# Front of a linear-attention and routed-MoE kernel: results in a ring of two double banks, denominators as a 65th column, v cast by its load

## The chip, the cores and the metric

One NeuronCore of a Trainium2 chip runs the whole program. The metric is device time in microseconds, the median of three runs. Beside it stands one execution taken with the hardware profiler; all durations, waits and orders below are from that one. Engines are named as in the profile: PE is TensorE's matmul side and PEld its weight load, DVE is VectorE, ACT ScalarE, POOL GpSimd, SP the engine that only issues transfers.

## What is computed

Inputs q, k, v are (8, 8, 576, 64) fp32: 8 batches, 8 heads, 576 positions, 64 wide. The output of the attention, with the heads side by side, is 4608 tokens of 512, and goes through 8 experts whose weights per token come from eight rounds of row and column normalisation.

```python
def phi(x):
    return np.where(x > 0, x, np.exp(x) - 1.0) + 1.0
q_p, k_p = (phi(q), phi(k))
kv = np.einsum('bhsd,bhse->bhde', k_p, v)
z = np.sum(k_p, axis=2)
num = np.einsum('bhsd,bhde->bhse', q_p, kv)
den = np.einsum('bhsd,bhd->bhs', q_p, z)[..., None] + 1e-06
...
x = transposed(num / den)                  # (4608, 512)
P = np.exp(x @ w_gate - max)
for _ in range(8):
    P /= P.sum(1, keepdims=True) + 1e-09
    P /= P.sum(0, keepdims=True) + 1e-09
    P *= N / E
for e in range(E):
    out += P[:, e:e + 1] * (np.maximum(x @ w1[e], 0.0) @ w2[e])
```

## The kernel before

The program has two parts that overlap. The *front* computes the attention; the *experts* are the two matmul layers of the eight experts.

**Front.** The function `att(b, g)` (from L268) handles one *half batch*: four heads of one batch, numbered n = 2b + g from 0 to 15. Its steps, with the names of the profile:

- three loads into `kqin` (k and q) and `vin`, 576 KB each, two buffers deep (L283 to L298). Half batches 2 to 5 load through POOL's queue, the others through SP's.
- phi of k and q: exp on ACT into `e`, then on DVE max(x + 1, 1) into `t` and the minimum with `e` (L307, L320, L323).
- v is cast to fp16 into `vv`, whose 65th column is one, by ACT or DVE (L337). So the product k'v carries the sum of k' with it.
- `kv`: 18 matmuls into a double PSUM bank (L352); ACT or DVE evict it to `kvz`, masked to its diagonal blocks (L363, L365).
- `qt`: nine transposes of q' in two pieces of five and four (L380), copied out to `qpT` (L251 or L253).
- `den`: ten matmuls of two columns (L395); DVE adds epsilon and takes the reciprocal into `rden` (L401, L403).
- `num`: ten matmuls of 128 columns in three pieces (L419), each scaled by DVE with `rden` into `xn` (L424).
- `xt`: ten transposes of `xn` in two pieces (L435), copied out to `xT`, the tokens in the layout in which the experts read them (L439).

After each pair of batches 36 small matmuls make the gate's logits (`logits`, L447) and ACT their exp. When all are there, `sinkhorn` (L464) does the eight rounds on DVE, with one small matmul each (L493).

**PSUM.** The pools at L174 to L176 and L203 hold two single banks for layer 2 (`ye0`, `ye1`), two for layer 1 (`hq`), two that all of the front's results but `kv` share (`att`), and one double bank for `kv`. The first half batch borrows the `ye` banks for numerators. When the front is over, `f_close` (L563) frees its pools, and two fixed banks (`Zt`) take the place of the double bank.

**Experts.** Expert 0 runs alongside the front: tokens in nine groups of 512, layer 1 as plain matmuls for the first five groups (`layer1`, L608), ReLU on ACT, layer 2 in `unit_plain` (L877). The other groups, and all of experts 1 to 7, use a seven-product scheme with sums of blocks (`block7`, L755 and L760; `unit`, L1015). The blocks of x for it are formed on DVE (`x_blocks`), written to DRAM (`xd`) and read back per expert (`xs`). Weights are loaded and cast to fp16 through POOL's queue (`load_w`, L236), two buffers each for w1 and w2.

**Order.** Nothing is left to a scheduler at run time. Every step is registered with `add` or `fadd` and gets a number; at the end a list gives, engine by engine, the numbers in the order in which they are issued (L1116 to L1177). Each engine works its list in order, waiting at each step for its data and its buffer, so a step that waits holds up all that follow it on its engine. TensorE's list starts with dummy matmuls on a zeroed tile (`warm`, L527), which fill the time until inputs arrive. Costs beside `add` are for the planner that made the list and do nothing on the chip; so do dependencies that carry no data.

Of the kernel before, what the change touches and what calls it, by code (L numbers as in the profile page):

```python
# [10 lines left out]
FP32 = mybir.dt.float32  # L11
FP16 = mybir.dt.float16
# [127 lines left out]
def kernel(  # L140
# [10 lines left out]
    nc = tc.nc  # L151
# [24 lines left out]
    aps = ctx.enter_context(tc.tile_pool(name="aps", bufs=2, space=PSUM))  # L176
# [9 lines left out]
    NX = 5  # L186
    MG = 99
# [14 lines left out]
    vv_t = [fp.tile([P, 2, NJ, D + 1], FP16, tag=f"vv{i}", name=f"vv{i}", bufs=1) for i in range(2)]  # L202
    kvps = front.enter_context(tc.tile_pool(name="kvps", bufs=1, space=PSUM))  # L203
    diag = fp.tile([P, 2, D + 1], FP16, tag="diag", name="diag", bufs=1)
    half_ = fp.tile([P, 2], FP32, tag="half", name="half", bufs=1)
    p_kv = S_.pool(1)
# [3 lines left out]
    p_vv, p_kvz, p_qpT, p_xn, p_rden = (S_.pool(2) for _ in range(5))  # L210
# [50 lines left out]
    v_land, kv_id = [], []  # L261
# [6 lines left out]
    def att(b, g):  # L268
# [3 lines left out]
        def ps_home(i):  # L272
            if n < 1 and i < 2:
                return p_ye[i], yps, f"ye{i}"
            return p_att, aps, "att"

# [3 lines left out]
        for nm, ten in (("k", k), ("q", q), ("v", v)):  # L280
            gr = gin[nm] = S_.grp(p_in[nm]) if nm == "v" else gkq

            def fn(_, gr=gr, nm=nm, ten=ten):  # L283
                if nm == "v":
                    gr["tile"] = fp.tile([P, 2, NJ, D], FP32, tag="vin", name="vin", bufs=2)
                    dst = gr["tile"]
                else:
                    if nm == "k":
                        gr["tile"] = fp.tile([P, 2, 2, NJ, D], FP32, tag="kqin", name="kqin", bufs=2)
                    dst = gr["tile"][:, "kq".index(nm)]  # L290
                (nc.gpsimd if 2 <= n <= 5 else nc.sync).dma_start(
                    out=dst.rearrange("p r j d -> p r (j d)"),
                    in_=AP(tensor=ten.tensor, offset=(b * H + 4 * g) * S * D, ap=src))
            ti = fadd(("pool", 1.0) if 2 <= n <= 5 else ("sp", 0.45), fn, acq=[] if nm == "q" else [gr],
# [43 lines left out]
        tvv.append(fadd({"act": 1.15, "dve": 0.76}, f_v, deps=[ta, tin["v"]],  # L338
# [8 lines left out]
        def f_kv(_):  # L347
            gkv["tile"] = kvps.tile([P, 2, 512], FP32, tag="kv", name="kv_ps")
            for j in range(NJ):
                for hh in range(2):  # L350
# [3 lines left out]
                                     rhs=gvv["tile"][s, :, j, :], start=(j == 0), stop=(j == NJ - 1))  # L354
        kv_id.append(len(S_.t))
        tkv = fadd(("pe", 0.54), f_kv, deps=[tph["k"]] + tvv, acq=[gkv], use=[gvv, gt["k"]], prio=pr)
# [17 lines left out]
        for j0, j1 in ((0, 5), (5, NJ)):  # L374
            gp = S_.grp(p_att)

            def f_qt(_, j0=j0, j1=j1, gp=gp):
                gp["tile"] = aps.tile([P, 5, 2, PW], FP16, tag="att", name="qt_ps")
                for j in range(j0, j1):
                    nc.tensor.transpose(gp["tile"][:, j - j0, :, :].rearrange("p h w -> p (h w)"),  # L380
                                        gt["q"]["tile"][:, j, 2:4, :].rearrange("p r d -> p (r d)"), ident)

            def f_qc(e, j0=j0, j1=j1, gp=gp):
                copy(e, gq["tile"][:, :, j0:j1, :].rearrange("p h j w -> p j h w"), gp["tile"][:, 0:j1 - j0])
            t1 = fadd(("pe", 0.06 * (j1 - j0)), f_qt, deps=[tph["q"], tqa, t_init], acq=[gp], use=[gt["q"]], prio=pr)
# [3 lines left out]
        gden, grd, gxn = S_.grp(p_att), S_.grp(p_rden), S_.grp(p_xn)  # L389

        def f_den(_):
            gden["tile"] = aps.tile([P, 5, 2, 2], FP32, tag="att", name="den_ps")
            for i, j in enumerate(js):
                for hh in range(2):
                    nc.tensor.matmul(gden["tile"][:, i, :, hh],  # L395
                                     lhsT=gq["tile"][:, hh, j:j + 2, :].rearrange("p j w -> p (j w)"),
                                     rhs=gz["tile"][:, hh, :, D], start=True, stop=True)

        def f_rd(_):
            grd["tile"] = fp.tile([P, 5, 4], FP32, tag="rden", name="rden")  # L400
            nc.vector.tensor_scalar(out=grd["tile"], in0=gden["tile"].rearrange("p i r h -> p i (r h)"),  # L401
                                    scalar1=1e-6, scalar2=None, op0=ALU.add)
            nc.vector.reciprocal(grd["tile"], grd["tile"])  # L403
        tden = fadd(("pe", 0.26), f_den, deps=tq + tz, acq=[gden], use=[gq, gz], prio=pr)
        trd = fadd(("dve", 0.5), f_rd, deps=[tden], acq=[grd], use=[gden], prio=pr)

        def f_xa(_):
            gxn["tile"] = fp.tile([P, 5, 4, D], FP16, tag="xn", name="xn")
        txa = fadd(("none", 0.0), f_xa, deps=[tden], acq=[gxn], prio=pr)
        txn = []  # L410
        for i0, i1 in ((0, 2), (2, 4), (4, 5)):
            hn = ps_home(i0 // 2)
            gn = S_.grp(hn[0])

            def f_num(_, i0=i0, i1=i1, gn=gn, hn=hn):
                gn["tile"] = hn[1].tile([P, 2, 2, 2, D], FP32, tag=hn[2], name="num_ps")
                for i in range(i0, i1):
                    for hh in range(2):
                        nc.tensor.matmul(gn["tile"][:, i - i0, :, hh, :],  # L419
                                         lhsT=gq["tile"][:, hh, js[i]:js[i] + 2, :].rearrange("p j w -> p (j w)"),  # L420
                                         rhs=gz["tile"][:, hh, :, 0:D], start=True, stop=True)

            def f_xn(_, i0=i0, i1=i1, gn=gn):
                nc.vector.tensor_tensor(  # L424
                    out=gxn["tile"][:, i0:i1], in0=gn["tile"][:, 0:i1 - i0].rearrange("p i r h e -> p i (r h) e"),
                    in1=grd["tile"][:, i0:i1, :, None].broadcast_to([P, i1 - i0, 4, D]), op=ALU.mult)
# [783 lines left out]
```

## Time and profile before

| | us |
|---|---|
| three runs | 959.27, 959.45, 959.61 |
| median | 959.45 |
| profiled execution, whole | 958.96 |
| its span, first to last instruction | 957.0 |
| last matmul issued at | 952.6 |
| logits of the last batches | 129 |
| first matmul of expert 0 | 20.0 |

The page lists each engine's busy time, a chain of waits followed back from the last instruction, and groups of equal instructions. A group's row reads: line, engine, operation, output and input tiles with shapes, count, then total busy time and mean ns of one, then the engine's idle time just before and what ended it. A row in the order of time has start and length in us, then the same names, and in brackets the idle time before it. Matmuls are pipelined, so a row of several is longer than the distance to the next row; the distance between two starts is what the engine was held for.

### The profile page before, as it was taken

What the parts mean: (1) busy time and instruction counts of PE and PEld (TensorE: products, weight loads), DVE (VectorE), ACT (ScalarE), POOL (GpSimd) and SP (SyncE); (2) the same over time, 40 slices, a digit from 0 to 9 for tenths busy, and PEclk for the clock granted to TensorE, in tenths of its full rate; (3) what the DMA queues carried; (4) which work ended last, traced back from release to release, by engine and by line L of the source; (5) the groups of instructions that cost most, each with busy time, mean ns of one, the idle gap of its engine ahead of it and who ended that gap; (6) DMA issues with size and microseconds to landing.
All of it is one profiled execution on the core that took longest, in us unless ns stands there. A gap on an engine that the chain in (4) does not pass through costs nothing.

```text
span 957.0 us, 18776 instructions
## 1 busy us (share of the span) xinstructions
PE 950.7 (99%) x7265; PEld 649.8 (68%) x7265; DVE 768.8 (80%) x1526; ACT 571.7 (60%) x1035; POOL 152.5 (16%) x199
## 2 busy tenths in 40 slices
PE   9999999999999999999999999999999999999998
PEld 4566676566676667766676666766677666766676
DVE  6898888788887787888877788877878788877776
ACT  6798854667555555555555555555555555555552
POOL 3100000012112211221112211221112211111111
PEclk9999999999999999999999999999999999999999
DMA  9987855533345421544135431644225431425545
GB/s 315 310 313 257 217 155 169 133 88 89 89 140 118 108 71 52 121 111 100 56 99 110 110 88 47 149 103 108 61 61 112 111 99 57 138 78 155 154 105 133
DMA packets 109946, 121.83 MB, mean 127 GB/s; under 512 B 7840, under 2 KB 92960, under 8 KB 109856
## 3 DMA queue, kind: packets, MB, share of 16 engines
q1 hardware_dynamic: 84320, 96.23, 32.6%
q0 software_dynamic: 25136, 23.87, 14.5%
q8 instruction: 57, 0.93, 0.4%
q10 hardware_dynamic: 400, 0.52, 0.2%
q14 instruction: 33, 0.27, 0.1%
HBM read 119.69 MB, written 17.69 MB: 144 GB/s over the span
## 4 chain that ended last, share of the span: by engine, by line
PE 97%; DMA 1%; DVE 1%; ACT 1%; issue 0%; SPq 0%; DVEq 0%
PE ye L1015 34%; PE hq L755 20%; PE att L755 10%; PE ye L877 7%; PE Zye L1015 6%; PE Zye L755 5%; PE hq L760 4%; PE hq L608 3%; PE att L760 2%; PE Zye L760 1%; PE xt_ps L435 1%; PE kv_ps L352 1%; PE num_ps L419 1%; DMA kqin<-in_q_dram 1%; PE qt_ps L380 1%; PE lg_ps L454 0%
## 5 line engine op out<-in xcount | busy, mean ns | idle before, releaser
L1029 DVE SCALAR_TENSOR_TENSOR acc<-ye,P_sb,acc 128x256 f32<-128x256 f32 x620 | 267.1, 478 | 104.6 <-PE ye L1015 102.4
L1015 PEld LDWEIGHTS <-S 128*128 128x128 f16 x1984 | 194.1, 98 | 45.9 <-issue 0.2
L1039 POOL TENSOR_TENSOR acc<-acc,h 128x256 f32<-128x256 f32 x124 | 102.8, 847 | 602.7 <-ACT h L1036 599.2
L1015 PE MATMUL ye<-h,S 128*128 128x256 f16 x1488 | 192.8, 273 | 0.0
L1015 PEld LDWEIGHTS <-h 128*128 128x128 f16 x1488 | 145.6, 98 | 40.0 <-issue 0.2
L795 ACT ACTIVATE h<-hq 128x512 f16<-128x512 f32 x134 | 80.1, 598 | 138.9 <-PE hq L755 122.3
L755 PEld LDWEIGHTS <-W 128*128 128x128 f16 x896 | 87.6, 98 | 81.4 <-issue 0.4
L755 PE MATMUL att<-xs,W 128*128 128x512 f16 x448 | 133.2, 379 | 0.0
L755 PE MATMUL hq<-xs,W 128*128 128x512 f16 x448 | 133.2, 379 | 0.0
L755 PE MATMUL hq<-xs,w 128*128 128x512 f16 x448 | 124.1, 379 | 0.0
L798 DVE CUSTOM_DVE_ANT_0 h<-att,s 128x512 f16<-128x512 f32 x126 | 86.5, 687 | 23.1 <-ACT s L782 22.6
L755 PEld LDWEIGHTS <-w 128*128 128x128 f16 x672 | 65.8, 98 | 54.8
L792 ACT ACTIVATE h<-Zye 128x512 f16<-128x512 f32 x134 | 80.1, 597 | 34.5 <-PE Zye L755 26.7
L1036 ACT ACTIVATE h<-Zye,P_sb 128x256 f32<-128x256 f32 x124 | 52.5, 471 | 76.9 <-PE Zye L1015 74.9
L798 DVE CUSTOM_DVE_ANT_0 h<-hq,s 128x512 f16<-128x512 f32 x126 | 86.5, 687 | 13.7 <-PE hq L755 13.7
L782 ACT COPY s<-hq 128x512 f32<-128x512 f32 x126 | 73.5, 583 | 35.3 <-PE hq L755 31.2
L775 ACT COPY Zye<-hq 128x512 f32<-128x512 f32 x134 | 77.9, 581 | 24.2 <-PE hq L755 18.9
L986 DVE TENSOR_TENSOR S<-h 128x1024 f16<-128x1024 f16 x124 | 85.2, 687 | 5.0 <-ACT h L795 5.0
L789 ACT COPY s<-att 128x512 f32<-128x512 f32 x126 | 74.5, 591 | 0.6 <-PE hq L755 0.6
L877 PE MATMUL ye<-w,h 128*128 128x512 f16 x296 | 73.5, 379 | 0.0
L755 PE MATMUL Zye<-xs,w 128*128 128x512 f16 x224 | 66.6, 379 | 0.0
L1015 PE MATMUL ye<-h,h 128*128 128x256 f16 x496 | 64.3, 273 | 0.0
(119 smaller groups left out, 1095.9 us busy)
## 6 DMA issues: line engine op xcount, KB each, us to landing
xs<-xd SPq DMA_DIRECT2D x196, 256.0 KB, 4.0
w<-in_moe_w_dram POOLq DMA_DIRECT2D x48, 256.0 KB, 4.2
out_dram<-acc SPq DMA_DIRECT2D x67, 128.0 KB, 2.4
kqin<-in_k_dram SPq DMA_DIRECT2D x12, 576.0 KB, 5.2
kqin<-in_q_dram SPq DMA_DIRECT2D x12, 576.0 KB, 6.6
vin<-in_v_dram SPq DMA_DIRECT2D x12, 576.0 KB, 7.2
xs<-xd SPq DMA_DIRECT2D x49, 128.0 KB, 2.5
xd<-xT SPq DMA_DIRECT2D x27, 128.0 KB, 2.8
```

The lines of the kernel that those rows point to most:

```text
L755: nc.tensor.matmul(dst, lhsT=lhs(0, c), rhs=X(b)(c), start=(first and c == 0), stop=(c == 1), skip_group_check=True)
L775: nc.scalar.copy(out=Zt[1], in_=gX["tile"])
L782: nc.scalar.copy(out=gs2["tile"], in_=gX["tile"])
L789: nc.scalar.copy(out=gs5["tile"], in_=gR["tile"])
L792: nc.scalar.activation(out=hd(0, 0), in_=Zt[1], func=AF.Relu)
L795: nc.scalar.activation(out=hd(1, 0), in_=gX["tile"], func=AF.Relu)
L798: nc.vector._custom_dve(TENSOR_ADD_SAT, out=dst, in0=ps, in1=sb, s0=3.0e38, s1=0.0)
L877: nc.tensor.matmul(gy[tt]["tile"], lhsT=hx(f, P * tt, P), rhs=gw2["tile"][:, f, :], start=(f == 0), stop=(f == NFT - 1))
L986: nc.vector.tensor_tensor(out=gS[i]["tile"], in0=a0, in1=a1, op=op)
L1015: nc.tensor.matmul(bank(g_)[:, s, :], lhsT=lhs(s, kk), rhs=rhs(kk), start=(new and s == 0 and kk == 0), stop=(kk == 3), skip_group_check=True)
L1029: nc.vector.scalar_tensor_tensor(out=dst(), in0=bank(g_)[:, s, :], scalar=P_sb[:, gg, e:e + 1], in1=dst(), op0=ALU.mult, op1=ALU.add)
L1039: nc.gpsimd.tensor_tensor(out=dst(), in0=dst(), in1=gst["tile"], op=ALU.add)
```

## The change

- One pool of two double banks (`kv`, tiles from `pair_tile`) takes all of the front's TensorE results: `kv`, `qt`, numerators, `xt` and logits, in the order of TensorE's list. The pool `att` is opened only when the front closes, and `sinkhorn`'s matmuls wait for that. The dummy matmuls use a `ye` bank.
- The denominator matmuls are gone. The numerators' right-hand side is the whole of `kvz`, 65 columns per head, 130 in all, and the 65th column of the result is the denominator. It is read from PSUM with a stride, by DVE or ACT, to add epsilon; DVE then takes the reciprocal.
- Numerators come in two pieces (three and two of the five position blocks) in place of three. From half batch 2 on `qt` and `xt` are one piece each in place of two.
- From half batch 2 on v is loaded through POOL's queue as fp16, cast by the transfer; the copy into `vv` is then fp16 to fp16. Rows of `vv` are 66 wide in place of 65.
- Nine dummy matmuls fewer (38 in place of 47), and three pieces of expert 0's first layer stand ahead of the last transposes of half batch 1.
- The lists of all engines are new. On POOL ten more v loads stand in the queue, and expert 1's w2 is loaded behind three parts of expert 2's w1, where before it stood ahead of expert 1's w1.

```diff
-    aps = ctx.enter_context(tc.tile_pool(name="aps", bufs=2, space=PSUM))
+    aps = [None]
...
+    VC = range(2, 2 * B)
...
-    vv_t = [fp.tile([P, 2, NJ, D + 1], FP16, tag=f"vv{i}", name=f"vv{i}", bufs=1) for i in range(2)]
-    kvps = front.enter_context(tc.tile_pool(name="kvps", bufs=1, space=PSUM))
+    vv_t = [fp.tile([P, 2, NJ, D + 2], FP16, tag=f"vv{i}", name=f"vv{i}", bufs=1) for i in range(2)]
+    kvps = front.enter_context(tc.tile_pool(name="kvps", bufs=2, space=PSUM))
...
-    p_kv = S_.pool(1)
+    p_kv = S_.pool(2)
+
+    def pair_tile(dt=FP32):
+        return kvps.tile([P, 2, 512 if dt == FP32 else 1024], dt, tag="kv", name="kv_ps")
...
-                    gr["tile"] = fp.tile([P, 2, NJ, D], FP32, tag="vin", name="vin", bufs=2)
+                    gr["tile"] = fp.tile([P, 2, NJ, D], FP16 if n in VC else FP32, tag="vin", name="vin", bufs=2)
...
-                (nc.gpsimd if 2 <= n <= 5 else nc.sync).dma_start(
+                (nc.gpsimd if 2 <= n <= 5 or (nm == "v" and n in VC) else nc.sync).dma_start(
...
-            gkv["tile"] = kvps.tile([P, 2, 512], FP32, tag="kv", name="kv_ps")
+            gkv["tile"] = pair_tile()
...
-        for j0, j1 in ((0, 5), (5, NJ)):
-            gp = S_.grp(p_att)
+        for j0, j1 in ((0, 5), (5, NJ)) if n < 2 else ((0, NJ),):
+            gp = S_.grp(p_kv)
...
-        def f_den(_):
-            gden["tile"] = aps.tile([P, 5, 2, 2], FP32, tag="att", name="den_ps")
-            for i, j in enumerate(js):
-                for hh in range(2):
-                    nc.tensor.matmul(gden["tile"][:, i, :, hh],
-                                     lhsT=gq["tile"][:, hh, j:j + 2, :].rearrange("p j w -> p (j w)"),
-                                     rhs=gz["tile"][:, hh, :, D], start=True, stop=True)
...
-        for i0, i1 in ((0, 2), (2, 4), (4, 5)):
-            hn = ps_home(i0 // 2)
-            gn = S_.grp(hn[0])
+        for i0, i1 in ((0, 3), (3, 5)):
+            ni = i1 - i0
+            gn, grd = S_.grp(p_kv), S_.grp(p_rden)
...
-                        nc.tensor.matmul(gn["tile"][:, i - i0, :, hh, :],
+                        nc.tensor.matmul(gn["tile"][:, hh, 2 * D1 * (i - i0):2 * D1 * (i - i0 + 1)],
                                          lhsT=gq["tile"][:, hh, js[i]:js[i] + 2, :].rearrange("p j w -> p (j w)"),
-                                         rhs=gz["tile"][:, hh, :, 0:D], start=True, stop=True)
+                                         rhs=gz["tile"][:, hh].rearrange("p r e -> p (r e)"), start=True, stop=True)
...
+            def f_ra(eng, num=num, grd=grd, ni=ni):
+                o, i_ = grd["tile"][:, :, 0:2 * ni], num()[:, :, :, D]
+                if eng == "act":
+                    nc.scalar.activation(out=o, in_=i_, func=AF.Identity, bias=eps_t[:, 0:1])
+                else:
+                    nc.vector.tensor_scalar(out=o, in0=i_, scalar1=1e-6, scalar2=None, op0=ALU.add)
+
+            def f_rd(_, grd=grd, ni=ni):
+                nc.vector.reciprocal(grd["tile"][:, :, 0:2 * ni], grd["tile"][:, :, 0:2 * ni])
...
-        for c2 in range(2):
-            gx = S_.grp(p_att)
+        for c0, c1 in ((0, 1), (1, 2)) if n < 2 else ((0, 2),):
+            gx = S_.grp(p_kv)
...
-        gl = S_.grp(p_att)
+        gl = S_.grp(p_kv)
...
-            c = add(("pe", 0.2), f_c, deps=[a], acq=[gc], prio=-200.0, lat=0.15)
+            c = add(("pe", 0.2), f_c, deps=[a, t_close], acq=[gc], prio=-200.0, lat=0.15)
...
+        aps[0] = ctx.enter_context(tc.tile_pool(name="aps", bufs=2, space=PSUM))
...
-        pool 0 50 106 108 110 112 114 144 146 148 179 181 185 187 189 219 600 221 223 577 632 629 1617 1619 1137 1139
-        1621 1623 1163 1262 1626 1628 1630 1632 1165 1260 1286 1288 1383 1385
+        pool 0 50 106 108 110 112 114 140 142 144 171 173 177 179 544 181 207 209 211 241 271 303 333 363 393 425 455
+        485 515 525 573 1561 1563 1565 576 1083 1570 1567 1081 1107 1109 1206 1572 1574 1204 1230 1576 1232 1327 1329
+        1353
...
```

In POOL's new list 241 to 515 are the v loads of half batches 6 to 15, 573 is expert 1's w1, 1561, 1563 and 1565 are parts of expert 2's w1, and 576 is expert 1's w2. The lists of the other engines, as long as before, are left out.

## What the change should do to the time

> **What bounds the kernel now.** I read the page's head and its chain of waits first, then the table of stretches, then TensorE's order of time.
>
> ```profile
> span 957.0 us, 18776 instructions
> PE 950.7 (99%) x7265; PEld 649.8 (68%) x7265; DVE 768.8 (80%) x1526; ACT 571.7 (60%) x1035; POOL 152.5 (16%) x199
> ...
> PE 97%; DMA 1%; DVE 1%; ACT 1%; issue 0%; SPq 0%; DVEq 0%
> ```
>
> ```profile
> core 0: us, PE busy (x) PEld busy (x) DVE busy (x) ACT busy (x) POOL busy (x), PEclk, DMA share, GB/s
> 0.00:20.00 20.00, 18.52 (x162) 9.89 (x163) 12.39 (x32) 11.46 (x15) 8.28 (x17) 1.00 0.98 300
> 20.00:41.00 21.00, 20.26 (x193) 11.52 (x193) 16.78 (x31) 15.34 (x23) 5.01 (x7) 1.00 1.09 326
> 41.00:130.00 89.00, 89.00 (x1075) 56.75 (x1069) 79.50 (x168) 71.26 (x112) 1.84 (x3) 1.00 0.77 241
> ```
>
> The first row is the start: inputs arrive and TensorE idles on dummy matmuls. From 41 us on its row has no gap at all, so a matmul taken out there shortens the run by its issue distance, unless a new wait fills the hole. VectorE is next: 79.50 of 89.00 us, with 9.5 us to spare for the whole stretch, and it is what the new order leans on. From 20 to 41 us the DMA share is above one: there the arrival of inputs decides.
>
> A busy row can hide a half-rate TensorE, so I looked at the distances themselves:
>
> ```profile
> 43.51 0.41 PE L395 MATMUL den_ps<-kvz,qpT 128*128 128x2 f16 x10
> 43.77 1.02 PE L608 MATMUL hq<-xT,w 128*128 128x512 f16 x4
> 44.63 0.28 PE L419 MATMUL num_ps<-kvz,qpT 128*128 128x128 f16 x2
> 44.75 1.02 PE L608 MATMUL hq<-xT,w 128*128 128x512 f16 x4
> 45.71 0.69 PE L352 MATMUL kv_ps<-vv,t 64*128 64x130 f16 x18
> 46.33 1.04 PE L877 MATMUL ye<-w,h 128*128 128x512 f16 x4
> ```
>
> Starts follow each other by work alone: ten denominators in 43.77 - 43.51 = 0.26 us, four 512-wide ones in 0.86, two numerators in 0.12, eighteen `kv` in 0.62.
>
> **The change, part by part.** *Denominators.* L395 goes: 16 half batches x 0.26 = 4.2 us of TensorE, of which 14 x 0.26 = 3.6 fall after the start. The 65th column makes a numerator matmul 130 columns wide instead of 128, at 60 ns each: 1.6% of 160 x 60 ns, 0.15 us (0 to 0.3). Nine dummy matmuls go from the start; they stand in waits for inputs and are worth nothing.
>
> *Evictions.* VectorE's and ScalarE's work in the front, from the groups by shape up to 131 us:
>
> ```profile
> L323 DVE TENSOR_TENSOR t<-t,e 128x1152 f16<-128x1152 f16 x32 | 23.9, 750 | 2.4 <-ACT e L307 1.9
> L424 DVE TENSOR_TENSOR xn<-num_ps,rden 128x512 f16<-128x512 f32 x32 | 21.8, 688 | 4.1 <-PE num_ps L419 3.7
> L253 DVE COPY xT<-xt_ps 128x576 f16<-128x576 f16 x16 | 7.1, 453 | 1.8 <-PE xt_ps L435 1.6
> L424 DVE TENSOR_TENSOR xn<-num_ps,rden 128x256 f16<-128x256 f32 x16 | 6.6, 415 | 1.2 <-PE num_ps L419 1.1
> L363 ACT ACTIVATE kvz<-kv_ps,half 128x130 f16<-128x130 f32 x16 | 5.1, 382 | 0.5 <-PE kv_ps L352 0.5
> L253 DVE CAST vv<-vin 128x1152 f16<-128x1152 f32 x6 | 4.6, 766 | 0.0
> L403 DVE RECIPROCAL rden<-rden 128x20 f32<-128x20 f32 x16 | 4.5, 278 | 0.5
> L253 DVE COPY qpT<-qt_ps 128x640 f16<-128x640 f16 x8 | 3.9, 487 | 2.1 <-PE qt_ps L380 2.0
> L253 DVE COPY qpT<-qt_ps 128x512 f16<-128x512 f16 x8 | 3.4, 420 | 0.6 <-PE qt_ps L380 0.6
> L365 DVE TENSOR_TENSOR kvz<-kv_ps,diag 128x260 f16<-128x260 f32 x8 | 3.3, 418 | 1.6 <-PE kv_ps L352 1.4
> L401 DVE TENSOR_SCALAR rden<-den_ps 128x20 f32<-128x20 f32 x16 | 2.8, 174 | 1.6 <-PE den_ps L395 1.5
> ```
>
> VectorE before, of the kinds the change touches: 21.8 + 6.6 + 7.1 + 4.6 + 4.5 + 3.9 + 3.4 + 3.3 + 2.8 = 58.0 us. After: the scaling comes in pieces of 768 and 512 numbers; 256 more cost 688 - 415 = 273 ns, so 768 take 0.96, and 16 x (0.96 + 0.69) = 26.4. The epsilon is added 20 times on VectorE, 3.5 (twelve go to ScalarE, which needs no longer than 382/2 = 0.19 each), 32 reciprocals 8.9. `qpT`: four small copies, 1.8, and seven of 1152; 128 numbers more cost 487 - 420 = 67 ns, so 1152 take 0.487 + 4 x 0.067 = 0.76, 5.3 in all. `xT`: four of 576, 1.8, and six of 1152, 4.6. `kvz` six times, 2.5. The copy of a v that is already fp16 has no row. L323 reads two fp16 tensors and L253 one fp32 tensor, both 4608 bytes a partition, in 0.75 and 0.77; the copy reads half of that. So 0.38, with 0.77 as the dear end and a gain down to 0.3 not excluded; ten on VectorE, 3.8. Sum 58.6, or 0.6 us more than before, 4.5 more at the dear end. ScalarE casts four times less. With 9.5 us spare this does not bind as a total; it costs where a TensorE piece waits for one eviction.
>
> The Trainium skill, "VectorE: DVE Perf Modes", section "What auto-detection actually checks", says that a single-source copy of 16-bit data inside SBUF can move four elements a cycle; an estimate from that page for 1152 elements is 0.3 us plus overhead. By it the ten copies would take about 0.4 each and the sum stays; by the dear end VectorE's work grows by 3.9. No run here shows such a copy yet.
>
> *The ring.* This is the new wait. Before, `kv` had its own double bank and everything else two single banks. Now each `kv`, `qt`, numerator, `xt` and logits piece waits until the piece two before it is evicted, and all later matmuls queue behind it. I laid the pieces in the new order at the distances above and compared the work between a piece and its second successor with the shortest eviction: 0.2 us from TensorE to the copy, the copy itself, 0.06 back. The 0.2 comes from here: the piece behind an `xt` starts when that is issued, and its copy starts 0.20 later:
>
> ```profile
> 38.78 1.03 PE L877 MATMUL ye<-w,h 128*128 128x512 f16 x4
> ```
> ```profile
> 38.98 0.46 DVE L253 COPY xT<-xt_ps 128x576 f16<-128x576 f16 x1 [0.38 <-PE xt_ps L435]
> ```
>
> Half batches 2 and 3 come up short: between `kv[3]` and the first numerator of 3 stands one numerator (0.24) against 0.2 + 2 x 0.38 at most for ScalarE's pair of L363; `qt[3]` has 0.62 against 0.2 + 0.76; the numerators of 2 and 3, one behind the other, lack 0.2 to 0.4 each. Together some 1.2 us. From half batch 4 on the order keeps one to four 0.86-us pieces between, and the cover is met, but barely: more than twenty places have under 0.2 us to spare, and five (around the numerators of 12 and 13, both `xt` of 12 and 14, the last logits) lack 0.2 each, some 0.8 us together. So 2.0 us of new stalls; the low end is 0.8, if only the widest gap of each group counts; the high end, with 0.1 us for each of twenty tight places, 4.
>
> They replace these, which the order of before had in the same stretch:
>
> ```profile
> 23.62 0.68 PE L380 MATMUL qt_ps<-ident,t 128*128 128x128 f16 x9
> 24.52 0.69 PE L352 MATMUL kv_ps<-vv,t 64*128 64x130 f16 x18 [0.23 <-DVE vv L253]
> ...
> 30.49 0.40 PE L419 MATMUL num_ps<-kvz,qpT 128*128 128x128 f16 x4
> 31.08 0.41 PE L395 MATMUL den_ps<-kvz,qpT 128*128 128x2 f16 x10 [0.19 <-DVE kvz L365]
> 31.68 0.39 PE L419 MATMUL num_ps<-kvz,qpT 128*128 128x128 f16 x4 [0.19 <-DVE xn L424]
> ```
>
> Nine transposes need half a microsecond, so 24.52 is 0.4 late; 31.08 is 0.59 after 0.24 of work, 31.68 is 0.60 after 0.26: 0.4 + 0.35 + 0.34 = 1.1 us.
>
> *The start.* Three half-pieces of `hq` (0.43 each) move ahead of `xt[1]`, up to 1.3 us gained. Against it stands the ring: in half batch 1 `kv`, `qt`, both `xt` of 0 and the numerators follow each other with almost no other work, each waiting for an eviction. The pieces that need half batch 1 cannot come sooner than its chain, and half batch 2's data lands only at 19.8 (VectorE waits for it there, below), so I take 0, from -1.3 to +0.7.
>
> *Loads.* v from half batch 6 on leaves SP's queue for POOL's. The bytes read are the same and the copy into SBUF is halved.
>
> ```profile
> 19.79 0.76 DVE L320 TENSOR_SCALAR t<-kqin 128x1152 f16<-128x1152 f32 x1 [0.85 <-DMA kqin<-in_k_dram]
> ```
> ```profile
> vin<-in_v_dram SPq DMA_DIRECT2D x12, 576.0 KB, 7.2
> ...
> vin<-in_v_dram POOLq DMA_DIRECT2D x4, 576.0 KB, 11.6
> w<-in_moe_w_dram POOLq DMA_DIRECT2D x2, 1024.0 KB, 11.9
> ```
>
> The POOL loads of before stood in the stretch with a DMA share over one, behind weights; that is queueing. In the new order the engine that casts v has work of its own between the release of a v buffer and its next use: where one engine does both, 8.0 us at the least (ScalarE, half batch 8), 9.6 next (VectorE, 9), against 7.2. I take 0, a gain excluded because the weights set the first loads' order and the later ones have cover; the dear end is the second rival. On POOL ten v loads now stand ahead of expert 1's w1, and expert 1's w2 goes behind three parts of expert 2's w1, which wait for the last use of expert 0's w1. That is 27 us of TensorE work before w2's first use, against 11.9 for such a load and four issues of some 0.74: hidden.
>
> *Sum.* Of the ring's 2.0 I take 1.4: the 1.2 at half batches 2 and 3, where each wait stands behind the other, and the low end, 0.2, of the later 0.8, since there a stall of one place lengthens the cover of the next, and the old order ran from 41 to 130 us without a gap on a VectorE as full. So -3.6 + 0.15 + (1.4 - 1.1) + 0 = -3.15. The profiled execution ends at 958.96 us, of which 957.0 is the span; 958.96 - 3.15 = 955.8. The median of the three runs, 959.45, lies 0.5 above it: 956.3.
>
> **Rivals.** *The ring binds (959.0).* The tight places and the dear copy cost 4.1 us in place of 1.4, and most of the gain is given back: 956.3 + 2.7 = 959.0. For it: VectorE at 89% and twenty places without slack. Against: the old order was as full and did not stall.
>
> *Late v (963).* The other side. If the 11.6 us of POOL loads are the path's and not the queue's, each v comes 4.4 later than 7.2; with a cover of 8 to 9.6 us in the three tightest (half batches 8, 9, 10) each puts some 2 to 3 us into VectorE's or ScalarE's queue and from there into TensorE: 956.3 + 7 = 963. It decides from a v load of 8 us on, and crosses zero at about 10. Against it: POOL spends the same time on each issue whatever VectorE does.
>
> ```profile
> L291 POOL DMA_DIRECT2D vin<-in_v_dram x4: 704/726/739, 11.6 to 30.9; - x4
> ```
>
> The Trainium skill, "SBUF — State Buffer", section "SBUF: two separate sides", warns that a DMA issued from POOL stalls while VectorE holds the port pair both share, because POOL cannot write its descriptors; that speaks for this rival. The 704 to 739 ns above, with VectorE 80% busy (16.78 of 21.00), speak against, though they are issue times only.
>
> *The work does not leave.* The instruction lists show 160 matmuls fewer by the denominators and nine dummies, so this has no chance of its own.
>
> **How the numbers follow.** Forecast 956.3: 0.66; its own range is 954.2 (start 1.3 better, stalls 0.8) to 957.7 (stalls 1.4 more). Ring binds, 957.7 to 960: 0.18. Late v, 961 to 965: 0.10. Something after the front, expert 1's w2 for one, 960 to 965: 0.06. The range for eight in ten is 954.0 to 959.6, which leaves out the last two and a little of the second. 0.2% is 1.9 us, about what a measurement of this kernel tells from no change, so faster ends at 957.5: 0.65 of the first case and 0.01 of the second, 0.66. Slower begins at 961.4: late v and the last case, 0.16 with their few tenths below it made up by what I have not thought of. Same is the rest, 0.18.
>
> **What would show it.** Right: no L395 row, about 3.6 us less between 41 and 180 us, TensorE's waits in the front on `qpT`, `xn` and `kvz` releases summing to 2 us, v landing in 7 us or less, the copy at 0.4. Wrong: gaps of over 0.3 us again and again from half batch 4 on (ring), or VectorE or ScalarE waiting for `vin` (late v).

## The result, and the profile after

| | before | changed |
|---|---|---|
| seven runs of each, us | 958.89 to 959.61, median 959.27 | 955.26 to 958.01, median 956.19 |
| profiled execution | 958.96 | 956.11 |
| its span | 957.0 | 954.3 |

The ratio is 0.9971, with an interval of 0.9959 to 0.9982: faster by 1.7 to 3.9 us. Forecast were 956.3 for the median and 955.8 for the profiled execution.

The page's head and its chain of waits, then two of the stretches that were shown of the kernel before (busy time of PE, PEld, DVE, ACT and POOL, granted clock, DMA share, GB/s):

```profile
span 954.3 us, 18433 instructions
PE 944.9 (99%) x7096; PEld 643.8 (67%) x7096; DVE 770.4 (81%) x1528; ACT 565.9 (59%) x1024; POOL 161.2 (17%) x209
...
PE 95%; DMA 2%; DVE 1%; ACT 1%; issue 0%; SPq 0%; DVEq 0%; ACTq 0%
```
```profile
20.00:41.00 21.00, 19.80 (x174) 10.72 (x173) 17.88 (x33) 14.59 (x22) 5.99 (x8) 1.00 1.11 283
41.00:130.00 89.00, 88.44 (x981) 55.16 (x976) 80.42 (x167) 73.07 (x117) 7.35 (x11) 1.00 0.86 235
```

169 matmuls are gone: 160 denominators and nine dummies. TensorE is still the bound, but the row from 41 us is no longer without a gap: 88.44 of 89.00 us. TensorE's rows in order of time show where the gaps are:

```profile
28.80 0.69 PE L351 MATMUL kv_ps<-vv,t 64*128 64x130 f16 x18
29.71 0.93 PE L407 MATMUL kv_ps<-kvz,qpT 128*128 128x130 f16 x8 [0.22 <-DVE qpT L257]
30.48 1.02 PE L886 MATMUL ye<-w,h 128*128 128x512 f16 x4
31.34 0.51 PE L407 MATMUL kv_ps<-kvz,qpT 128*128 128x130 f16 x6
32.23 0.52 PE L407 MATMUL kv_ps<-kvz,qpT 128*128 128x130 f16 x6 [0.38 <-DVE xn L425]
...
75.47 0.40 PE L407 MATMUL kv_ps<-kvz,qpT 128*128 128x130 f16 x4
76.18 0.40 PE L407 MATMUL kv_ps<-kvz,qpT 128*128 128x130 f16 x4 [0.31 <-DVE xn L425]
...
88.19 1.03 PE L886 MATMUL ye<-w,h 128*128 128x512 f16 x4
89.46 0.66 PE L381 MATMUL kv_ps<-ident,t 128*128 128x128 f16 x9 [0.24 <-ACT kvz L363]
...
236.74 1.04 PE L1024 MATMUL ye<-w,S 128*128 128x256 f16 x8
238.17 1.02 PE L764 MATMUL hq<-xs,w 128*128 128x512 f16 x4 [0.40 <-DVE h L807]
```

By the distances of starts, less the work between (0.216 us for a 512-wide matmul, 0.11 for a 256-wide one, 0.058 for a numerator, 0.62 for eighteen `kv`), TensorE stood 0.29 us ahead of the first eight numerators, 0.31 inside them at 30.25, 0.54 at 32.23, 0.48 at 76.18, 0.41 at 89.46 and 0.56 at 238.17. The 0.40 that an expectation below gives for the first of these counts as a wait the 0.1 us that TensorE takes behind the last `kv` everywhere. The brackets name what came last: but for the last row it is an eviction or copy out of the ring (`qpT`, `xn`, `kvz`), in the form that the prediction gave; the last waits for an add-and-ReLU on VectorE, long after the front.

To add up stages of two different orders I counted, in each trace, TensorE's useful work from the first row on (every matmul at its undisturbed distance, without dummies and without the old denominators; 933.8 us in both kernels), and noted the time at which a given amount had been issued. The last row is the end of the last matmul's issue. Both kernels were profiled a second time (below), so there are two traces of each:

| useful work | before | before again | changed | changed again | change of the mean |
|---|---|---|---|---|---|
| start to 6 us of work | 21.50 | 21.86 | 20.97 | 21.01 | -0.7 |
| 6 to 25 | 21.10 | 21.11 | 21.08 | 21.15 | 0.0 |
| 25 to 110 | 88.47 | 88.56 | 86.17 | 85.95 | -2.45 |
| 110 to the last matmul | 821.68 | 821.87 | 821.75 | 821.77 | 0.0 |
| last matmul | 952.75 | 953.39 | 949.97 | 949.88 | -3.15 |

The second row ends at 42 to 43 us of time, the third at 128 to 132. So in these traces the gain lies in the front, with a part at the very start that was not forecast. The stages are not independent of each other, as the part on why the forecast held shows.

### The profile page after: what moved, and what is told of

Same layout as the page of the kernel before. It is cut to its first block, busy times and chain, and to the rows that moved or that the text cites. A ratio compares the mean times of both kernels' runs of the same rounds, so it can differ in the third digit from the quotient of the medians.

```text
span 954.3 us, 18433 instructions
## 1 busy us (share of the span) xinstructions
PE 944.9 (99%) x7096; PEld 643.8 (67%) x7096; DVE 770.4 (81%) x1528; ACT 565.9 (59%) x1024; POOL 161.2 (17%) x209
## 4 chain that ended last, share of the span: by engine, by line
PE 95%; DMA 2%; DVE 1%; ACT 1%; issue 0%; SPq 0%; DVEq 0%; ACTq 0%
PE ye L1024 34%; PE hq L764 20%; PE att L764 10%; PE ye L886 6%; PE Zye L1024 6%; PE Zye L764 5%; PE hq L769 4%; PE hq L618 3%; PE att L769 2%; DMA kqin<-in_k_dram 2%; PE Zye L769 1%; PE kv_ps L440 1%; PE kv_ps L351 1%; PE kv_ps L407 1%; PE kv_ps L381 1%; ACT e L306 1%
```

## The experiments

Each kernel ran beside the kernel before, whose median was 959.4 (first four), 959.76 (next four), 959.68 (next three) and 959.52 (last). "Front" is the time between 25 and 110 us of useful work, by the count above.

| run | median, range, executions | ratio to before, interval | front |
|---|---|---|---|
| changed again | 955.45, 955.33 to 956.01, 5 | 0.9961, 0.9949 to 0.9974 | 85.95 |
| denominators back | 959.80, 958.94 to 960.49, 11 | 1.0004, 0.9995 to 1.0013 | 88.4 |
| order, half batches 2, 3 | 956.26, 955.72 to 958.53, 10 | 0.9972, 0.9963 to 0.9981 | 85.50 |
| order, four places | 955.89, 955.18 to 956.87, 5 | 0.9966, 0.9953 to 0.9978 | 85.35 |
| v fp32, by SP | 956.13, 955.61 to 956.42, 5 | 0.9962, 0.9949 to 0.9974 | 85.60 |
| v fp32, by POOL | 956.11, 955.67 to 958.34, 5 | 0.9966, 0.9954 to 0.9979 | 85.62 |
| v copied twice | 956.39, 956.31 to 957.04, 5 | 0.9964, 0.9951 to 0.9978 | 86.22 |
| order, three places | 955.56, 955.14 to 956.60, 5 | 0.9959, 0.9946 to 0.9971 | 86.31 |
| no late dummies | 955.79, 955.58 to 956.67, 5 | 0.9962, 0.9950 to 0.9975 | 85.97 |
| three places, q 14 first | 955.60, 954.96 to 957.11, 5 | 0.9961, 0.9947 to 0.9974 | 85.87 |
| the same, v fp32 by SP | 955.53, 955.07 to 956.23, 5 | 0.9957, 0.9944 to 0.9969 | 85.43 |
| before again | 959.71, 959.09 to 960.22, 11 | 1.0001, 0.9992 to 1.0010 | 88.56 |

### The changed kernel again

> The changed kernel once more, unaltered. If its seven runs (955.26 to 958.01, against 958.89 to 959.61 for the kernel before) spread by chance from run to run, the median comes to 956.2 +- 0.5 and the profile shows the same stalls of TensorE at the same places (0.40 and 0.31 us at 29.7 and 30.3, 0.54 at 32.2, 0.48 at 76.2, 0.41 at 89.5, 0.56 at 238.2). If the stalls hang on when loads land, those at 76 and 89 (behind which exp on ScalarE and phi on VectorE had waited for kqin) come out different by some tenths, while those at 29.7 to 32.2, whose waits are evictions, stay.

The median of the five, 955.45, lies below the 955.7 to 956.7 that was expected; all twelve executions of the changed kernel together have a median of 955.88. The stalls at 30 to 32 us came again within a hundredth (0.29, 0.32, 0.54), the one at 238 too; that at 76 was 0.70 in place of 0.48, and that at 89 was gone. So the first are set by the order of evictions, and those at 76 and 89 move from one execution to the next.

### Denominators back

```diff
+                if i0 == 0:
+                    for i, j in enumerate(js):
+                        for hh in range(2):
+                            nc.tensor.matmul(gn["tile"][:, hh, 400 + 2 * i:402 + 2 * i], lhsT=...,
+                                             rhs=gz["tile"][:, hh, :, D], start=True, stop=True)
```

> The ten denominator matmuls of each half batch are issued again, ahead of the first numerators and into columns of their tile that nobody reads; all else is the changed kernel. If removing them is what gained 3.6 us (14 half batches after the start at 0.26, nothing in the start), this is 3.0 to 3.6 us slower than the changed kernel: 959.2 to 959.8, no faster than the kernel before, and a little of the added time falls into waits that are there anyway (29.7, 76.2). Rival: the gain came from the start (0.5 us earlier there) and from the loads, and the new order has holes enough for 160 small matmuls: under 1.5 us slower, below 957.7.

Its group in the front, and a stretch of TensorE's rows:

```profile
L408 PE MATMUL kv_ps<-kvz,qpT 128*128 128x2 f16 x160 | 6.5, 165 | 0.8 <-ACT kvz L363 0.6
```
```profile
31.81 0.51 PE L413 MATMUL kv_ps<-kvz,qpT 128*128 128x130 f16 x6
32.43 0.42 PE L408 MATMUL kv_ps<-kvz,qpT 128*128 128x2 f16 x10
32.71 0.51 PE L413 MATMUL kv_ps<-kvz,qpT 128*128 128x130 f16 x6
```

Ten of them hold TensorE 32.71 - 32.43 = 0.28 us, about as before the change. With them the kernel takes 959.8, 3.9 us more than the changed kernel and no less than the kernel before (interval 0.9995 to 1.0013). The profiled execution, 959.02, lies 3.0 above the mean of the changed kernel's two (956.11 and 956.01). That is the whole gain: by this run everything else in the change comes to about nothing.

The trace also shows what became of the holes. The six numerators at 31.81 take 0.35, so TensorE stands 0.27 at 32.43, where the changed kernel stood 0.54; the stalls at 76 and 89 us, which differ from one execution to the next, are not there. Between 25 and 110 us of useful work, which leaves denominators out, this kernel took 88.4 us, 2.4 more than the mean of the changed kernel's two traces, for 3.1 of denominators. So some of the denominators had stood in waits for other engines, and without them TensorE is idle there.

### One place in the order: half batches 2 and 3

```diff
- pe ... 638 160 130 636 639 637 138 ...
+ pe ... 638 160 636 130 639 637 138 ...
```

> TensorE's list alone: half of one layer-2 tile (four matmuls, 0.86 us) is issued between the first numerators of half batch 3 and those of 2, which stall 0.54 us for the ring at 32.2 us; the half tile behind them moves up by it. If that stall is on the path that sets the end, the stall goes and the end comes 0.4 to 0.54 us earlier: 955.7. Rival: what the numerators feed (xt of 2, then the experts' first layer) is the path, the stall reappears there behind the later numerators: 956.2, no change.

```profile
32.06 1.02 PE L886 MATMUL ye<-w,h 128*128 128x512 f16 x4
32.92 0.51 PE L407 MATMUL kv_ps<-kvz,qpT 128*128 128x130 f16 x6
33.27 1.89 PE L886 MATMUL ye<-w,h 128*128 128x512 f16 x8
35.90 0.90 PE L440 MATMUL kv_ps<-ident,xn 128*128 128x128 f16 x13 [0.74 <-DVE xn L425]
```

The stall of 0.54 is gone, and 0.91 us stand in front of the transposes of `xn` instead (1.73 of work from 33.27, then 35.90). The time stayed. Here VectorE's chain from numerators to `xn` is the path, and filling a hole with work that would have run anyway only moves the hole: the rival was right at this place.

### Four places, three places

```diff
- pe ... 323 353 717 ...   702 406 727 ...
+ pe ... 323 717 353 ...   702 727 406 ...
- dve ... 1222 1299 ...
+ dve ... 1299 1222 ...
```

> The edit of the run before, and three more swaps of neighbours: a first-layer piece ahead of the last numerators of half batch 9 (stall 0.48 at 76.2), one ahead of the transposes of 11 (0.41 at 89.5), and on VectorE an add-and-ReLU ahead of one sum of blocks (0.56 at 238.2). If each stall is TensorE time and nothing refills the holes, 2.0 us less: 954.2. If VectorE's chain between pieces sets the pace in the front (the rival in which the ring binds), the three stalls of the front come back elsewhere and only the 0.56 after it is won: 955.6.

> The three later swaps of the run with four, without the move at half batches 2 and 3, where the profile showed the stall of 0.54 come back as 0.91 in front of the transposes of xn. If the three stalls are TensorE time that nothing refills, 0.48 + 0.41 + 0.56 less than the changed kernel: 954.5. If they are refilled as at half batches 2 and 3, no change: 955.9.

Neither 954.2 nor 954.5 came. In both runs the stalls at 76, 89 and 238 us are gone. From 110 us of work on, all four kernels with the swap on VectorE's list took 821.19, the others that differ from the changed kernel only elsewhere 821.75 to 821.77: those 0.56 us are won and nothing refills them. The front gained in the first (85.35), not in the second, because of a single new stall:

```profile
101.92 1.03 PE L618 MATMUL hq<-xT,w 128*128 128x512 f16 x4
103.94 1.21 PE L351 MATMUL kv_ps<-vv,t 64*128 64x130 f16 x36 [0.99 <-ACT xT L255]
```
```profile
100.66 1.16 ACT L306 ACTIVATE e<-kqin 128x1152 f16<-128x1152 f32 x1 [1.43 <-DMA kqin<-in_q_dram]
```
```profile
88.21 0.37 SPq L290 DMA_DIRECT2D kqin<-in_k_dram  x1
91.38 0.34 SPq L672 DMA_DIRECT2D xd<-acc  x1
91.76 1.24 SPq L290 DMA_DIRECT2D kqin<-in_q_dram  x1
```

Read from the last fence (SP's issues) upwards: the load of q 14 was issued 3.55 us after that of k 14, behind a store in the new list of SP; it landed 8.9 us later, ScalarE waited 1.43 us for it, and TensorE stood 1.16, 0.1 of which a step into `kv` takes anyway. The medians, 955.89 and 955.56, are not told apart from the changed kernel's 955.88.

### q 14 ahead of the store

```diff
- sp ... 481 595 483 588 ...
+ sp ... 481 483 595 588 ...
```

> The run with three swaps, and on SP's queue the load of q of half batch 14 one place earlier, ahead of a store of x blocks that waits for its data until 91.4 us. In the run with three that q landed at 100.6, 8.9 us after its issue, ScalarE and VectorE waited 1.43 and 0.83 us for it and TensorE 0.99 us (1.16 with the gap of its pieces) at 103.9. If the store's place in the queue made it late, q is issued at about 88.6 and lands by 96, the stall is gone in every execution, and the runs lie at 954.6 to 955.2 with none above 956. If the landing is late because several transfers share the engines at that time, it lands late still and the time is that of the run with three, 955.6.

> The same swaps and the same move of q 14, on the kernel that loads v as fp32 through SP as before the change. If the loads' way is worth nothing, the time is that of the run just before it within 0.4 us, and the spread tells whether late transfers come with POOL's queue: all runs within 1 us here, one or two some 2 us above the rest with POOL's v loads.

q 14 was issued at 88.69 and landed at 93.76, and the stall at 103.9 is gone, so the place in the queue had made it late. It doesn't show in most executions: of the ten profiles with the old place two have a stall there, 1.16 and 0.32 us, the two of the changed kernel none. The time did not follow: 955.6, one execution at 957.1. With v by SP the median is 955.53, the lowest profile of all (953.3 of span) and a range of 1.2 us. Against the kernel before it is faster (0.9944 to 0.9969); that it beats the changed kernel isn't shown by the times, though in the lists of TensorE's waits from 20 us to the end it has 1.2 us against 1.9: the 0.48 and 0.41 us at 76 and 89 and the 0.56 at 238 are gone from it, those at half batches 2 and 3 stay.

### The loads of v

```diff
  by SP:
-    VC = range(2, 2 * B)
+    VC = ()
- sp ... 237 239 267 269 ...
+ sp ... 237 239 241 267 269 271 ...
  by POOL:
-   gr["tile"] = fp.tile([P, 2, NJ, D], FP16 if n in VC else FP32, tag="vin", ...
+   gr["tile"] = fp.tile([P, 2, NJ, D], FP32, tag="vin", ...
```

> v is loaded as before the change: fp32, half batches 2 to 5 through POOL's queue and 6 to 15 through SP's, each behind its q; the copy into vv casts again. All else is the changed kernel (955.9 over its twelve runs so far, 955.3 to 958.0). The prediction's term for the loads is 0: 955.4 to 956.4, with VectorE's ten copies back at 0.77 us in place of 0.45, 3.2 us more work in its spare time. Rival 1, the loads through POOL cost something (they land in 8.3 us, k and q in 6 to 7): 0.5 to 1.5 us faster, and the spread of the runs back to under 1 us, as it was before the change. Rival 2, VectorE is the bound of the front: 1.5 to 3 us slower.

> v through POOL's queue as in the changed kernel, but as fp32, cast by the copy into vv. Against the run before it tells the queue from the cast. If what makes the loads slow is POOL's queue and order, v lands as late as with the cast (about 8 us) and the time is that of the changed kernel, 955.9 +- 0.5. If it is the cast in the transfer (q0 took about as much of the 16 engines' time for half the bytes), v lands in 6 to 7 us here and the time is 0.3 to 1 us shorter.

Both take the time of the changed kernel. From half batch 6 on v landed 7.4 us after its issue with the cast, 7.1 as fp32 by POOL and 7.0 as fp32 by SP (means of ten), so neither the cast nor the queue makes much of it. What the transfers cost the 16 DMA engines from 42 to 102 us is in the queue's row (packets, MB, share), first of the changed kernel, then of fp32 by POOL:

```profile
q0 software_dynamic: 2717, 2.95, 32.7%
```
```profile
q0 software_dynamic: 1440, 5.90, 27.4%
```

2.95 MB are ten loads of 288 KB, and 32.7% of 60 us is 19.6: by these rows the packets of a cast load held the engines for 1.96 us, those of an fp32 load, with twice the bytes written, for 1.64. The front's 85.6 in both fp32 kernels stands against 86.17 and 85.95, but the order runs reached 85.35 with the cast, so a cost of the cast of some tenths is not shown. Of 52 executions with v by POOL's queue seven lay above 957 us, of ten with v by SP none; that is too few to say that the queue widens the spread.

### Each copy of v on VectorE twice

```diff
             copy(e, gvv["tile"][:, :, :, 0:D], gin["v"]["tile"])
+            if e == "dve":
+                copy(e, gvv["tile"][:, :, :, 0:D], gin["v"]["tile"])
```

> Every copy of v that VectorE makes is made twice: 0.45 us more on VectorE in ten half batches of the front, 4 to 4.5 us in all, with no other change. By the prediction VectorE has 9 us to spare from 41 to 130 us and the total does not bind: TensorE's stalls grow by at most a fifth of it, 0 to 0.9 us slower, 955.9 to 956.8. Rival (the ring binds): each added piece stands between a TensorE piece and its second successor and most of it comes out as stalls, 2.5 to 4 us slower, 958.4 to 960.

```profile
41.00:130.00 89.00, 88.56 (x983) 54.95 (x981) 83.67 (x175) 72.41 (x116) 8.19 (x12) 1.00 0.86 233
```

VectorE was busy for 83.67 us in the stretch instead of 80.42, and TensorE as long as before. 4.5 us of added VectorE work cost 0.5 by the median and some 0.6 by the stages (0.45 of it before 42 us of time, where VectorE's chain is the path). VectorE as a total does not bind.

### Dummies

```diff
-        ... n=2 if 12 <= i < 16 else 1: f_warm(e, n)
+        ... n=2 if 12 <= i < 16 else 1 if i < 25 else 0: f_warm(e, n)
```

> The changed kernel without its last nine dummy matmuls (those between 14 and 21 us; 1.9 us of TensorE). By the prediction dummies stand in waits for inputs and evictions and are worth nothing: the pieces of half batch 1 start where they did behind the last landing of its v, and the time is that of the changed kernel, 955.9 +- 0.5. Rival 1, they overshoot: pieces follow directly behind them at 18.9, 19.8 and 16.1 without idle time, so up to 0.6 us faster. Rival 2, TensorE's granted clock falls when it idles there: the clock of the first slices under 1.00 and over 1 us slower.

```profile
20.25 2.47 PE L618 MATMUL hq<-xT,w 128*128 128x512 f16 x10
23.43 0.81 PE L618 MATMUL hq<-xT,w 128*128 128x512 f16 x3 [0.71 <-ACT h L622]
```
```profile
13.00:20.00 7.00, 5.31 (x62) 3.18 (x60) 6.22 (x15) 1.81 (x3) 3.79 (x6) 1.00 1.16 290
```

Six us of work were done at 20.47, half a microsecond earlier than in the changed kernel though its loads landed 0.4 later, so these dummies did overshoot. But the next wait, for ReLU on ScalarE at 23.43, took all of it back, and twelve us of work were done at 27.46, against 26.98 and 27.09. The granted clock stayed at 1.00 with TensorE idle for 1.7 of 7 us (second fence). No change, as forecast.

### The kernel before again

> The kernel before once more, unaltered, for a second trace of it. In the twelve profiles of the changed kernel and its variants the last load of half batch 1 landed at 12.20 to 12.81 us, and work done by a given amount (six us of TensorE work counted from the start) came 8.7 us after it in all that kept the dummies; the changed kernel's landed at 12.25, that of the one profile of before at 12.75. If the half microsecond by which the changed kernel's trace leads at the start is only the loads, this profile has the same 8.7 us behind its own landing, and its time less that landing is 946.2 +- 0.3, against 943.8 for the two profiles of the changed kernel. If the new order made the start faster, the distance is 0.3 us or more longer here.

The first two rows of TensorE in this profile; the same rows of the first profile of before; then rows of the changed kernel:

```profile
1.33 8.25 PE L527 MATMUL yw<-warm 128*128 128x512 f16 x24 [1.33 <-DVE warm L515]
9.43 0.67 PE L380 MATMUL qt_ps<-ident,t 128*128 128x128 f16 x9
```
```profile
1.33 7.63 PE L527 MATMUL yw<-warm 128*128 128x512 f16 x24 [1.33 <-DVE warm L515]
8.80 0.67 PE L380 MATMUL qt_ps<-ident,t 128*128 128x128 f16 x9
```
```profile
6.73 1.46 PE L536 MATMUL yw<-warm 128*128 128x512 f16 x6
8.35 0.40 PE L381 MATMUL kv_ps<-ident,t 128*128 128x128 f16 x4 [0.15 <-POOL gate L342]
```

The supposition behind this run held for the first profile of before and fell for this one. In the first, six us of work came 8.75 us behind the landing of half batch 1's v at 12.75, as in the changed kernel (8.72 and 8.73, behind 12.25 and 12.28): there the changed kernel led by as much as its loads. Here v landed at 12.43, and six us of work still came later, 9.43 us behind it; in the kernels with the changed order and all of its dummies that distance was 8.7 to 9.0.

The reason is in the first rows. Before, 24 dummies stood ahead of the first transposes, without a pause, and the transposes start the moment the last is issued. How long they take isn't fixed: the first ones follow each other at 0.427 us and the later ones at 0.216, and the step came after 11 dummies in one profile and after 14 in the other, 3 x 0.21 = 0.63 us, just the 9.43 - 8.80 between the two. The changed kernel has 20 there, and TensorE stands idle ahead of its first transposes (0.15 us, in brackets). Whether late transposes held up anything else is in ScalarE's rows, of this profile and then of the first:

```profile
9.85 0.58 ACT L251 COPY qpT<-qt_ps 128x512 f16<-128x512 f16 x1 [0.71 <-PE qt_ps L380]
```
```profile
12.78 1.16 ACT L251 CAST vv<-vin 128x1152 f16<-128x1152 f32 x1 [0.17 <-DMA vin<-in_v_dram]
```

Here ScalarE waited 0.71 us for the transposes, and began to cast half batch 1's v at 12.95, 0.52 after it had landed. In the first profile it did not wait for them, and it had time left to wait for v itself. So the dummies were on the path in one of the two profiles. No run puts the four back into the changed kernel.

## Why the forecast held, step by step

The number was right; of its terms two were not, with opposite signs, so that it came this close is in part luck.

- *Denominators, -3.6.* Right within what the runs tell: -3.0 by the profiles of the run with them back, -3.9 by the medians.
- *130 columns instead of 128, +0.15.* Nothing to be seen. Six numerators take 0.35 us here and two took 0.12 before:

```profile
73.40 0.51 PE L407 MATMUL kv_ps<-kvz,qpT 128*128 128x130 f16 x6
73.75 1.02 PE L618 MATMUL hq<-xT,w 128*128 128x512 f16 x4
```

- *Ring, +1.4 against 1.1 of old stalls.* At half batches 2 and 3 the 1.2 forecast was 0.29 + 0.31 + 0.54 = 1.14, at the three places named. The old stalls were read a little wrong: 0.1 of the 0.4 at 24.52 is what a step from transposes to `kv` takes elsewhere (14.06 in the same trace), and 0.28 at 28.41 was left out; against that one stands a new wait of 0.55 for phi (`t`) at 28.18, which is no wait for the ring. The later part was mis-sized: of 0.8 found I had taken 0.2, because "a stall of one place lengthens the cover of the next". In the two traces it was about 0.7 (3.1 us of denominators gone between 25 and 110 us of work, 2.45 gained), and the run with the denominators back gave the same (3.1 put back, 2.4 lost). Some of it came by another way than the one argued: the stall at 89 us stood behind an exp that had waited 1.05 us for k 13, landed 8.3 us after its issue:

```profile
86.19 1.16 ACT L306 ACTIVATE e<-kqin 128x1152 f16<-128x1152 f32 x1 [1.05 <-DMA kqin<-in_k_dram]
```

  Between 6 and 25 us of work 0.5 of denominators went and nothing was gained. So new stalls less old ones come to +1.2, not +0.3. They are not the ring's alone: the denominators had stood in part of them. The rival in which the ring binds gave 3.0 and was too dear; one place of it, 30 to 36 us, was shown by the swap that only moved the hole.
- *Start, 0 (-1.3 to +0.7).* It was -0.7 in the mean of the traces: -0.53 in the first pair, of which 0.50 is that half batch 1's v landed earlier, and -0.85 in the second, of which 0.70 is the shorter distance behind that landing. The step that failed is "nine dummy matmuls go from the start; they stand in waits for inputs and are worth nothing". The four of them that stood ahead of the first transposes held up ScalarE in the second profile of before, and not in the first. The distances in the order of time would have told that they might: the transposes followed the dummies without a gap, and a dummy that stands in a wait is followed by one. For the later dummies the step held, by the run without them. How much of the 0.7 reaches the end is open. With v as fp32 by POOL six us of work were done at 21.54, 0.57 later than in the changed kernel, and the last matmul came at the same time within 0.02 us: what the start lost, the front had made up.
- *VectorE's work.* Forecast were 58.6 us for the kinds touched; they took 56.3. The main rows that replace the old ones:

```profile
L425 DVE TENSOR_TENSOR xn<-kv_ps,rden 128x768 f16<-128x768 f32 x16 | 15.1, 947 | 0.4
L425 DVE TENSOR_TENSOR xn<-kv_ps,rden 128x512 f16<-128x512 f32 x16 | 11.0, 688 | 0.5
L257 DVE COPY qpT<-kv_ps 128x1152 f16<-128x1152 f16 x7 | 5.3, 755 | 2.1 <-PE kv_ps L381 2.0
L255 ACT COPY vv<-vin 128x1152 f16<-128x1152 f16 x4 | 4.7, 1172 | 0.0
L257 DVE COPY vv<-vin 128x1152 f16<-128x1152 f16 x10 | 4.5, 454 | 0.0
L422 DVE RECIPROCAL rden<-rden 128x12 f32<-128x12 f32 x16 | 3.5, 223 | 0.3
L422 DVE RECIPROCAL rden<-rden 128x8 f32<-128x8 f32 x16 | 3.1, 192 | 0.3
```

  0.96, 0.69 and 0.76 were forecast for the first three. The fp16 copy took 0.454 on VectorE, between the bounds and near the 0.38 taken; on ScalarE it took 1.17, no less than a cast from fp32 (1.15 before and after). The shorter reciprocals took 0.22 and 0.19 where I had left them at 0.28. Adding the epsilon on ScalarE took 0.27 to 0.28, more than the 0.19 that I had read off a row of another operation. The "four elements a cycle" of the Trainium skill ("VectorE: DVE Perf Modes", "What auto-detection actually checks"), an estimate of 0.3 us and overhead, agrees with the 0.454.
- *Late v.* The loads came in time where it counted. The median of the fourteen by POOL is 8.3 us, but for half batches 8 to 10, the tight ones, it was 6.6, 5.5 and 7.4; of the ten that the change moved to POOL, only those of 12, 13 and 15 took longer than 8 (8.8 to 9.7). The sign that was named for being right, 7 us or less, came for four of the ten. Who waited for `vin`, in all of the changed kernel:

```profile
L290 POOL DMA_DIRECT2D vin<-in_v_dram x14: 696/708/852, 12.1 to 93.8; - x14
...
who waited for it (us, times):
  POOL vin L290: 49.9, 9
  POOL gate L342: 14.5, 2
  ACT vv L255: 0.6, 2
  PE kv_ps L381: 0.2, 1
```

  The sign by which this rival was to be known, VectorE or ScalarE waiting for `vin`, is there for the two fp32 copies of the start alone; POOL had nothing else to do. The issues took 0.70 to 0.85 us, 0.71 in the median, with VectorE at 80 of 89 us, so the stall that the Trainium skill ("SBUF — State Buffer", "SBUF: two separate sides") warns of cost them little. That it is absent isn't shown: the longest, from 93.77 to 94.62, ended 0.14 us after a piece of `t` on VectorE (93.72 to 94.48), and with v as fp32 by POOL one of 1.10 us, from 70.08, ended 0.15 after such a piece (70.27 to 71.03). v as fp32 by either queue ran in the same time: the term of 0 for the loads was right.
- *After the front.* Expert 1's w2 kept nobody waiting. The 0.56 at 238 us came from VectorE's new list, as the swap showed, and was balanced by shorter waits before it: 821.8 in both kernels.

In the prediction's terms the traces give -3.6 + 1.2 - 0.7 = -3.1, against -3.15 forecast. The 1.2 is what the stages leave over, so this sum is no check of the split. The two errors, 0.9 and 0.7, cancelled by chance; the range held both.

## What to carry to other kernels

Where one engine is the bound without gaps, the work taken from it is the term to start from, and the waits that replace it are the uncertain one: their places could be found by laying the new order at the old distances, their sum only within a factor. Some of the work taken out had itself stood in another engine's wait, and its hole stays open: of 3.1 us taken from the front 2.45 were gained. A stall that ends with a long chain on another engine isn't cured by filling it with work that would have run anyway; look for the swap on the other engine's list, as at 238 us. Filler is surely free only where the piece behind it still shows idle time in the order of time.

## What the runs showed of the hardware

- TensorE's first matmuls ran at half pace, 0.427 us in place of 0.216 for a 512-wide one, though the page's clock row says full speed, and for a time that differs from one execution to the next: 7 to 14 dummies in the fourteen profiles, until 4.2 to 7.3 us. The Trainium skill ("TensorE: Matmul & The Clock Gate", "What's actually happening") says that the same kernel shows 6, 11 or 14 such matmuls; the traces agree. It puts the ramp's penalty under 1% of a typical kernel's span and advises against fitting a count. Where a fixed number of them stands ahead of the first real piece, that piece came 0.63 us later in one execution than in the other here.
- A load of v that casts fp32 to fp16 held the DMA engines longer (1.96 us, changed kernel) than the plain one with twice the bytes written (1.64, v as fp32 by POOL).
- A copy of 1152 fp16 numbers in SBUF took 0.454 us on VectorE, against 0.754 with an fp32 source; on ScalarE both took 1.15 to 1.17.
